# Contractions over 448 rows on TensorE: three full chunks and two half chunks that share one slot

## The chip, the cores and the metric

One core of a Trainium2 chip runs the whole program. The metric is device time in microseconds (us) of one execution. Runs of different kernels are compared on the same chip in the same rounds. Engines are written as in the profile: PE is the matmul engine (TensorE), PEld its weight loads, DVE, ACT and POOL are the vector, scalar and general engines, SP issues most DMAs. "L667" is a line of the kernel file; the line numbers of two versions differ.

## The reference, cut to what matters

```python
x: (1, 2048, 448)            # bf16 everywhere
h  = x + attn(layernorm(x))  # 16 heads of 28; query s sees keys s, s-2, ..., s-14
# attn: qkv = xn @ wqkv (448 x 1344);  o @ wo (448 x 448)
z  = gelu(layernorm(h) @ w_in)        # 448 -> 1792
z1, z2 = z[..., :896], layernorm(z[..., 896:])
g  = w_sp (2048 x 2048) @ z2 + b_sp   # the spatial matmul
h2 = h + (z1 * g) @ w_out             # 896 -> 448
```

Five of these matmuls contract over 448 rows: q and k, V, the output projection of attention ("y" below), z2 and z1. One matmul instruction of this program contracts over at most 128 rows.

## The kernel before

The program is a list of tasks. A list scheduler inside the kernel file gives each task an engine and a place in that engine's order, from priorities and from cost formulas written in the file. What it emits is a fixed order per engine, with semaphore waits; an engine never skips a task that has to wait. PSUM is a pool of eight banks.

448 rows are cut into four chunks of 112. One task makes one output in one bank:

```python
DC = 112; NCH = 4
def qk_tile(tc, g8, prio):               # q or k of 512 tokens, four heads
    b = Buf(P_bank)
    G.add([("pe", pe_us(4, 512))], [
        lambda e, c=c: e.matmul(bank(b, 512), wsrc[:, c, gg, :], xhT[0:DC, c, col0:col0 + 512],
                                start=(c == 0), stop=(c == NCH - 1)) for c in range(NCH)], ...)
    G.add([("act", ...), ("dve", ...)], [... copy the bank to qT or kT ...])
# V of one attention block, y_block, a half of z2 and z1_tile are made the same way:
#   four matmuls of 112 rows, 448 columns (V, y, z2) or 512 columns (q, k, z1)

def att_block(i):                        # 18 blocks of 114 queries
    # V; scores: 16 matmuls of 32 rows, four at a time in the array (tile_position=(hh * 32, 0));
    # exp on ACT; mask on DVE; attention times V on PE; divide on DVE; transpose on PE
def y_block(m):                          # 16 blocks; ... then residual, layernorm, transposes
    G.add([("pe", pe_us(4, D))], [
        lambda e, c=c: e.matmul(bank(b, D), qT[0:DC, c, PAD + lo:PAD + hi], wo_sb[:, c, :],
                                start=(c == 0), stop=(c == NCH - 1)) for c in range(NCH)], ...)
```

The z2 matmuls may start only after the last attention block's first exponential (`after=[exps[-4]]`), the z1 matmuls only after its last one (`after=[last_exp]`), because ACT changes its function table there once (in the trace one table load of 1.28 us, at 91.19 us).

The softmax here doesn't subtract the row's maximum and nothing guards it: scores larger than these inputs give would overflow.

## Time and profile before

| | us |
|---|---|
| median of 4 runs | 265.51 (265.35 to 266.02) |
| span of the profiled run | 263.0 |
| PE busy | 255.1, 97% of the span |
| share of PE in the chain of waits | 89% |

From the page of the kernel before: busy time by engine, then the busy share (in tenths) of 40 slices of 6.6 us for PE, DVE, ACT and the granted PE clock, then the chain that ended last.

```profile
PE 255.1 (97%) x1868; PEld 129.8 (49%) x1868; DVE 152.4 (58%) x342; ACT 106.3 (40%) x204; POOL 46.6 (18%) x123
...
PE   6899999999998999999999999999999999999995
...
DVE  4697999979979999999431333131513133222233
ACT  1468979779979976772011000111010100010100
...
PEclk9999999999999999999999999999999999999999
...
PE 89%; DMA 3%; DVE 3%; ACT 2%; SPq 1%; POOL 1%; issue 0%; DVEq 0%
```

PE is the bound: it is busy in nearly every slice, and the chain of waits runs along it. DVE and ACT are nearly as busy until slice 17 (about 115 us), where attention and the z2 normalisation are over.

The next view gives busy time and instruction counts by stretches of time. I cut at four events seen in the trace: first transpose, first z2 matmul, first z1 matmul, end. So the lines are start, attention, z2, and the rest (z1, spatial matmul, last projection).

```profile
core 0: us, PE busy (x) PEld busy (x) DVE busy (x) ACT busy (x) POOL busy (x), PEclk, DMA share, GB/s
0.00:9.51 9.51, 7.38 (x29) 3.13 (x29) 4.23 (x14) 3.09 (x5) 7.09 (x31) 1.00 0.82 204
9.51:87.61 78.10, 75.53 (x961) 44.64 (x960) 70.76 (x163) 63.94 (x131) 22.80 (x51) 1.00 0.43 89
87.61:117.51 29.90, 29.90 (x212) 16.53 (x210) 29.73 (x77) 22.01 (x41) 12.45 (x32) 1.00 0.25 49
117.51:263.00 145.49, 142.31 (x673) 65.47 (x671) 47.73 (x92) 17.26 (x29) 4.27 (x11) 1.00 0.20 45
```

The price of a change of array mode can be read off PE's order of time (start, length, engine, line, operation; the ends of matmuls are modelled, the starts are what to read). The first line is the last of four full q/k matmuls, the second a group of 32-row score matmuls:

```profile
26.30 0.38 PE L524 MATMUL psum<-xhT,early 112*128 112x512 bf16 x1
26.62 0.38 PE L547 MATMUL psum<-qT,kT 32*128 32x114 bf16 x16
26.93 1.04 PE L524 MATMUL psum<-xhT,early 112*128 112x512 bf16 x4
```

A 512-column matmul that is followed by another of its kind has the next start 216 ns later; here it is 0.31 us. The whole score group takes 0.31 us; sixteen matmuls of 114 columns, four side by side, would stream in about 0.2 (their starts come in fours, 39 to 51 ns apart).

The last reading is the end of the attention stage, again in PE's order of time; the bracket is idle time of PE and what ended it. L535 is V, L547 the scores, L632 the first z2 matmul.

```profile
81.03 0.92 PE L535 MATMUL psum<-early,xhT 112*124 112x448 bf16 x4
...
82.27 0.38 PE L547 MATMUL psum<-qT,kT 32*128 32x114 bf16 x16
83.64 0.38 PE L547 MATMUL psum<-qT,kT 32*128 32x114 bf16 x16 [0.98 <-ACT E L556]
...
86.89 0.44 PE L547 MATMUL psum<-qT,kT 32*124 32x110 bf16 x16 [0.20 <-ACT E L556]
...
87.61 0.92 PE L632 MATMUL psum<-w_in,xhT 112*128 112x448 bf16 x4
```

After the last V block (81.03) three score groups remain, and PE begins z2 6.6 us later.

### The profile page before, as it was taken

To read this page: it belongs to the slowest core of one execution; us is meant where nothing else is said; L and a number is where in the kernel's file an instruction comes from. 1 tells how busy PE (TensorE), PEld (TensorE's weight loads), DVE (VectorE), ACT (ScalarE), POOL (GpSimd) and SP (SyncE) were. 2 spreads that over 40 slices of the span, in tenths; PEclk is the share of its full clock that TensorE was granted. 3 is DMA by queue.
4 is the path that set the end of the run, shared out by engine and by line. 5 is a ranking of instruction groups with operands and counts; after the bars stand their busy time and mean duration, and the time that the engine had idled before them with its cause. 6 is when DMAs were issued, how large, how long until landed. Compare 5 with 4: busy or idle time off the path is not lost.

```text
span 263.0 us, 4647 instructions
## 1 busy us (share of the span) xinstructions
PE 255.1 (97%) x1868; PEld 129.8 (49%) x1868; DVE 152.4 (58%) x342; ACT 106.3 (40%) x204; POOL 46.6 (18%) x123
## 2 busy tenths in 40 slices
PE   6899999999998999999999999999999999999995
PEld 2445665556655555554444444444544444444442
DVE  4697999979979999999431333131513133222233
ACT  1468979779979976772011000111010100010100
POOL 8676013221211125555000000000000000000000
PEclk9999999999999999999999999999999999999999
DMA  6999945000001213213000344401445200200002
GB/s 172 325 261 241 137 99 66 2 0 2 2 0 24 62 43 44 54 42 49 12 0 0 70 98 98 125 4 38 101 100 84 70 0 0 72 0 0 0 2 70
DMA packets 42182, 16.91 MB, mean 64 GB/s; under 512 B 35248, under 2 KB 41584, under 8 KB 42160
## 3 DMA queue, kind: packets, MB, share of 16 engines
q1 hardware_dynamic: 42160, 16.61, 29.3%
q8 instruction: 15, 0.25, 0.4%
q14 instruction: 7, 0.06, 0.1%
HBM read 6.37 MB, written 1.84 MB: 31 GB/s over the span
## 4 chain that ended last, share of the span: by engine, by line
PE 89%; DMA 3%; DVE 3%; ACT 2%; SPq 1%; POOL 1%; issue 0%; DVEq 0%
PE psum L667 37%; PE psum L524 10%; PE psum L632 9%; PE psum L654 9%; PE psum L685 8%; PE psum L596 4%; PE psum L535 4%; DMA x_tm<-in_A_x_dram 3%; PE psum L496 2%; PE psum L569 2%; PE psum L547 2%; ACT E L556 2%; PE psum L582 1%; DVE st L486 1%; DVE tring L491 1%; SPq L440 0%
## 5 line engine op out<-in xcount | busy, mean ns | idle before, releaser
L672 DVE TENSOR_TENSOR ub<-psum,bb 128x512 bf16<-128x512 f32 x28 | 19.4, 691 | 82.7 <-PE psum L667 82.7
L659 ACT ACTIVATE z1p<-psum 128x512 bf16<-128x512 f32 x28 | 16.7, 597 | 114.1 <-PE psum L654 114.1
L667 PE MATMUL psum<-wsp,z2p 128*128 128x512 bf16 x224 | 51.0, 379 | 0.0
L667 PE MATMUL psum<-early,z2p 128*128 128x512 bf16 x224 | 50.8, 379 | 0.0
L556 ACT ACTIVATE E<-psum 128x456 bf16<-128x456 f32 (+1 forms) x72 | 35.0, 562 | 1.4 <-PE psum L547 1.2
L667 PEld LDWEIGHTS psum<-wsp,z2p 128*128 128x128 bf16 x224 | 21.8, 98 | 26.5
L667 PEld LDWEIGHTS psum<-early,z2p 128*128 128x128 bf16 x224 | 21.9, 98 | 26.4
L524 PE MATMUL psum<-xhT,early 112*128 112x512 bf16 x128 | 30.5, 379 | 0.1
L654 PE MATMUL psum<-xhT,w_in 112*128 112x512 bf16 x112 | 28.8, 378 | 0.0
L514 POOL TENSOR_TENSOR rstd<-va,mhalf 128x1 f32<-128x1 f32 x48 | 27.7, 580 | 3.2
L512 POOL TENSOR_SCALAR va<-mv 128x1 f32<-128x1 f32 x48 | 13.2, 283 | 72.8 <-DVE mv L488 62.0
L632 PE MATMUL psum<-w_in,xhT 112*128 112x448 bf16 x128 | 25.5, 352 | 0.0
L685 PE MATMUL psum<-w_out,z1p 128*128 128x448 bf16 x112 | 21.8, 352 | 0.0
L486 DVE BATCH_NORM_STATS2 st<-x_tm 128x6 f32<-128x448 bf16 x32 | 19.2, 610 | 2.6 <-DMA x_tm<-in_A_x_dram 2.5
L637 ACT ACTIVATE z2p<-psum 128x448 bf16<-128x448 f32 x32 | 17.1, 544 | 7.2 <-PE psum L632 7.2
L564 DVE TENSOR_TENSOR E<-E,maskb 128x1824 bf16<-128x1824 bf16 (+1 forms) x18 | 19.6, 1089 | 0.0
L640 DVE BATCH_NORM_STATS2 st<-z2p 128x6 f32<-128x448 bf16 x32 | 18.1, 596 | 0.0
L654 PEld LDWEIGHTS psum<-xhT,w_in 112*128 112x128 bf16 x112 | 10.9, 97 | 13.3
L524 PEld LDWEIGHTS psum<-xhT,early 112*128 112x128 bf16 x128 | 11.5, 97 | 12.0 <-ACT V L508 0.2
L632 PEld LDWEIGHTS psum<-w_in,xhT 112*128 112x128 bf16 x128 | 12.1, 98 | 10.3
L535 PE MATMUL psum<-early,xhT 112*128 112x448 bf16 (+1 forms) x72 | 16.1, 352 | 0.8 <-DVE xhT L509 0.8
L685 PEld LDWEIGHTS psum<-w_out,z1p 128*128 128x128 bf16 x112 | 11.0, 98 | 10.4
(59 smaller groups left out, 245.7 us busy)
## 6 DMA issues: line engine op xcount, KB each, us to landing
out_dram<-tring SPq DMA_DIRECT2D x16, 112.0 KB, 1.8
w_in<-in_B_w_in_dram SPq DMA_DIRECT2D x1, 1568.0 KB, 13.8
x_tm<-in_A_x_dram SPq DMA_DIRECT2D x1, 896.0 KB, 10.0
early<-in_A_wqkv_dram SPq DMA_DIRECT2D x1, 784.0 KB, 6.0
w_out<-in_B_w_out_dram SPq DMA_DIRECT2D x1, 784.0 KB, 15.5
bb<-in_B_b_sp_dram SPq DMA_DIRECT2D x1, 512.0 KB, 13.2
wsp<-in_B_w_sp_dram SPq DMA_TRANSPOSE x32, 2.8
early<-in_B_w_sp_dram SPq DMA_TRANSPOSE x32, 2.7
```

Of the source, the lines that this page charges most:

```text
L486: G.add([("dve", dve_us(D))], [lambda e: e.bn_stats(st[:, s.slot, 0:6], x_tm[:, m, :])], [r_x[m]], [s], [s], prio=prio)
L514: G.add([("pool", 0.61)], [lambda e: e.tensor_tensor(rstd[:, k:k + 1], va[:, k:k + 1], mhalf[:, 0:1], ALU.pow)], [r_va[k], r_half], [r_rs[ ...
L524: lambda e, c=c: e.matmul(bank(b, 512), wsrc[:, c, gg, :], xhT[0:DC, c, col0:col0 + 512], start=(c == 0), stop=(c == NCH - 1)) for c in ra ...
L535: lambda e, c=c: e.matmul(bank(b, D, 0, nk), xhT[0:DC, c, t0:t0 + nk], stg[:, c, 2 * D:3 * D], start=(c == 0), stop=(c == NCH - 1)) for c ...
L556: lambda e, hh=hh: e.activation(E[0:nk, ev.slot, hh * 4:(hh + 1) * 4, 0:nq], bank(lb[hh], 512, 0, nk).rearrange("p (g c) -> p g c", c=128) ...
L564: lambda e: e.tensor_tensor(E[0:nk, ev.slot, :, 0:nq], E[0:nk, ev.slot, :, 0:nq], maskb[0:nk, mi:mi + 1, 0:nq].to_broadcast([nk, NHEAD, nq ...
L632: lambda e, c=c, b=b, h=h, m=m: e.matmul(bank(b, D), xhT[0:DC, c, PAD + 128 * m: PAD + 128 * m + 128], w_in[:, c, FH + D * h: FH + D * (h ...
L640: lambda e, h=h, m=m, s=s: e.bn_stats(st[:, s.slot, 6 * h:6 * h + 6], z2p[:, m, D * h:D * (h + 1)])],
L654: lambda e, c=c: e.matmul(bank(b, 512), w_in[:, c, fc * 128:(fc + 1) * 128], xhT[0:DC, c, PAD + 512 * tc: PAD + 512 * (tc + 1)], start=(c ...
L667: lambda e, s=s: e.matmul(bank(b, 512), z2p[:, s, fc * 128:(fc + 1) * 128], w[:, s, :], start=(s == 0), stop=(s == NB - 1)) for s in range ...
L672: G.add([("dve", dve_us(512))], [lambda e: e.tensor_tensor(ub[:, u.slot, :], bank(b, 512), bb[:, 512 * tc:512 * (tc + 1)], ALU.add)], [b, ...
L685: lambda e, f=f: e.matmul(bank(b, D), z1p[:, f, 128 * m:128 * m + 128], w_out[:, f, :], start=(f == 0), stop=(f == FC7 - 1)) for f in rang ...
```

## The change

448 is 3 x 128 + 64. The intent: make six full 128-row matmuls for two outputs, and put their two 64-row remainders into the upper and lower half of the array, at the same time. Two outputs take seven slots (a slot is the time of one full matmul: 216 ns with 512 columns, 189 with 448) where they took eight. One switch into the half-array mode and back is called a trip below. For that, q and k of one tile, two V blocks, the two halves of a z2 block and two z1 tiles become one task with two banks. Chunk 3 starts at row 320, so it overlaps chunk 2; each half of the array finds its 64 rows in place.

```diff
-DC = 112
+CH0 = (0, 128, 256, 320)
+        def pair(b, ws, xs, n, m=128):
+            fns = []
+            for j in range(2):
+                for c in (0, 1, 2 + j):
+                    fns.append(lambda e, j=j, c=c: e.matmul(bank(b[j], n, 0, m[j]), ws(j, ALL, c), xs(j, ALL, c),
+                                                            start=(c == 0), stop=False))
+            for j, ps, c in ((1, LO, 2), (0, HI, 3)):
+                fns.append(lambda e, j=j, ps=ps, c=c: e.matmul(bank(b[j], n, 0, m[j]), ws(j, ps, c), xs(j, ps, c),
+                                                               start=False, stop=True, tile_position=(ps.start, 0)))
+            return fns
+        def pair_us(n):
+            return pe_us(7, n) + 0.15
-                for isk in (0, 4):
-                    qk_tile(tc, g + isk, pos(4 * tc) - 3.0 + 0.3 * g)
+                qk_pair(tc, g, pos(4 * tc) - 3.0 + 0.3 * g)
  ... V: v_pair(i, ...) for blocks i and i + 1; z2: both halves of block m; z1: z1_pair for tiles tc and tc + 1 ...
         def y_block(m):
             G.add([("pe", pe_us(4, D))], [
-                lambda e, c=c: e.matmul(bank(b, D), qT[0:DC, c, PAD + lo:PAD + hi], wo_sb[:, c, :],
+                lambda e, c=c: e.matmul(bank(b, D), qT[HI if c == 3 else ALL, c, PAD + lo:PAD + hi],
+                                         wo_sb[HI if c == 3 else ALL, c, :],
  ... weights are loaded by two DMAs each (rows 0 to 383, rows 320 to 447); transposes make 128-row chunks ...
```

y has no partner for its remainder: its fourth matmul has 64 rows and a slot to itself. The scheduler is told seven slots and 0.15 us for a pair, and for y nothing beyond its four slots.

## The prediction

> **What bounds the kernel now.** PE: busy 97% of the 263.0 us span on the page, 89% of the chain of waits. Its busy times are modelled, so I took start-to-start times of neighbouring matmuls from the trace: 216 ns for 512 columns, 189 for 448, 56 for a transpose, the same at 112 contraction rows as at 128. Summed over the program's order this is about 244 us. The rest is mostly the start (first transpose at 9.5 us) and about 4 us of real idle time: 1.8 us before 14.7 us (x loads and DVE), 2.2 us at 82 to 88 us (ACT). From there to the end PE has no gap. DVE and ACT are 80 to 100% busy until about 90 us (windows of 10 us), but PE seldom waits for them.
>
> **What the change saves.** A pair of outputs took eight full slots; now six, plus one in which two 64-row matmuls run side by side. There are 30 pairs of 512 columns (16 q/k, 14 z1) and 25 of 448 (9 V, 16 z2): at best 30 x 216 + 25 x 189 ns = 11.2 us. That the halves overlap I take from the 32-row score matmuls, where four start within 10 ns.
>
> **What it adds.** The Trainium skill (TensorEngine Tiling (Array Packing), Tiling Modes, Key Properties) says that changing the tiling mode drains TensorE. The trace agrees and gives the price at the score matmuls: the last full matmul before them takes 312 ns to the next start instead of 216 (284 instead of 189); on the way back 138 ns where streaming takes 48; then 10 ns more in the first full matmul. One trip costs about 95 + 90 + 10 = 195 ns. Each pair makes one: a 512-column pair gains 20 ns, a 448-column pair loses 6. The output projection (L596, 16 blocks) gets a 64-row fourth chunk without partner: a full slot as before, plus a trip, 16 x 0.19 = 3.1 us lost. Four pairs run straight into score matmuls and share a switch (-0.4 us). Walking the changed PE order with these durations gives 246.6 against 244.3 us: **+2.3 us**, nearly all in the attention stage.
>
> **Other effects.** Weights load with 14% more bytes and one more issue each (0.45 us on the SP queue), so first weights and x blocks 4 to 7 land 0.5 to 1 us later, but q/k pairs now run earlier and fill PE's first waits. Both outputs of a pair finish together: evictions come in bursts, which may add stalls before 90 us; or the new order removes the wait at 82 us. I allow +0.2 us, spread about 2 us. Transposes, evictions, spatial matmul and last projection stay.
>
> **Prediction.** 268 us, 8 in 10 between 264.5 and 272. Faster by over 2%: 0.05; within: 0.80; slower: 0.15.
>
> **What would show it.** Trace: about 310 ns from a 512-column pair's last full matmul to its halves, 4 ns between the halves, 305 ns to the next full matmul; a pair 1.71 us against 1.73. Output projection 0.95 us per block against 0.76. PE gapless after 90 us; z2, z1 and spatial stages as long as before within 1 us.
>
> **What would make it wrong.** Halves not side by side (+11 us); a 64-row switch cheaper than a 32-row one (50 ns per trip is 3.5 us over 71 trips); PE starved in the attention stage by the new order.

## More of the kernel before

An execution of this program can have its TensorE clock halved for a few microseconds in the middle. The records show it as a mean granted clock of 0.981 to 0.987 (0.994 where it lasts half as long) instead of 0.998 to 1.000.

## The result, and the profile after

The changed kernel takes 276.1 us (median of 4, 275.51 to 276.11) against 265.51 before: 1.039 times as long, interval 1.037 to 1.041. (Ratios are the mean time of one kernel's fast runs over that of the other's in the same rounds, so not quite the ratio of the medians.) The prediction of 268, range 264.5 to 272, was wrong. The output is correct.

The page of the changed kernel, the same lines:

```profile
PE 260.7 (95%) x1846; PEld 119.8 (44%) x1868; DVE 158.4 (58%) x354; ACT 96.0 (35%) x192; POOL 45.0 (16%) x123
...
PE   6789999999998799999999999999999999999995
...
PEclk9999999999999779999999999999999999999999
...
PE 89%; DVE 5%; ACT 2%; issue 1%; POOL 1%; DVEq 0%; POOLq 0%
```

New here: the clock row falls to 7 tenths in two slices (13 and 14, 89 to 103 us), and PE is under 90% in slices 12 and 13 (82 to 96 us), where before it was so in slice 12 alone.

By stretches, cut at the same four events:

```profile
0.00:11.01 11.01, 8.88 (x28) 3.47 (x29) 3.96 (x13) 3.26 (x5) 7.37 (x31) 1.00 0.84 272
11.01:96.33 85.32, 77.84 (x952) 39.60 (x960) 76.27 (x174) 57.24 (x119) 19.93 (x50) 0.98 0.36 79
96.33:129.26 32.93, 32.77 (x211) 13.79 (x210) 29.95 (x77) 19.47 (x40) 12.96 (x32) 0.94 0.23 44
129.26:274.40 145.14, 141.23 (x659) 62.97 (x670) 48.25 (x93) 16.06 (x30) 4.75 (x11) 1.00 0.18 42
```

| stage | before, us | after, us | difference |
|---|---|---|---|
| start | 9.51 | 11.01 | +1.5 |
| attention | 78.10 | 85.32 | +7.2 |
| z2 | 29.90 | 32.93 | +3.0 |
| z1, spatial, last projection | 145.49 | 145.14 | -0.35 |

The last row has the 14 z1 pairs, and it moved as predicted (14 x 20 ns = 0.28 us). A z1 pair in PE's order of time:

```profile
152.34 1.46 PE L532 MATMUL psum<-xhT,w_in 128*128 128x512 bf16 x6
153.73 0.39 PE L535 MATMUL psum<-xhT,w_in 64*128 64x512 bf16 x2
154.06 1.25 PE L699 MATMUL psum<-wsp,z2p 128*128 128x512 bf16 x5
```

From its start to the next task's start are 1.71 us (predicted 1.71; two outputs took 1.73 before). Single starts in the trace give the parts: 310 ns from the last full matmul to the first half, 4 ns between the halves, 319 ns from there to the next full matmul, whose own successor comes 10 ns late. A 448-column pair takes 1.54 us (predicted 1.52, before 1.51), a y block 0.97 us against 0.76 (predicted 0.95). So the halves do run side by side, and the two mode switches cost nearly what the score matmuls said (319 ns on the way back, where 305 was predicted). That half of the prediction holds.

The end of the attention stage, where the time went (L579 scores, L601 attention times V, L532 full matmuls of pairs: V's at 80.81, z2's at 96.33):

```profile
80.81 1.31 PE L532 MATMUL psum<-early,xhT 128*128 128x448 bf16 x6
...
84.13 0.38 PE L579 MATMUL psum<-qT,kT 32*128 32x114 bf16 x16
...
86.29 0.38 PE L579 MATMUL psum<-qT,kT 32*128 32x114 bf16 x16 [0.30 <-DVE x_tm L632]
...
88.35 0.56 PE L601 MATMUL psum<-V,E 128*128 128x29 bf16 x16 [0.38 <-DVE E L596]
89.10 0.38 PE L579 MATMUL psum<-qT,kT 32*128 32x114 bf16 x16 [0.19 <-ACT E L588]
...
90.88 0.38 PE L579 MATMUL psum<-qT,kT 32*128 32x114 bf16 x16
91.99 0.56 PE L601 MATMUL psum<-V,E 128*128 128x29 bf16 x16 [0.73 <-DVE E L596]
...
95.20 0.67 PE L579 MATMUL psum<-qT,kT 32*124 32x110 bf16 x16
...
96.33 0.95 PE L532 MATMUL psum<-w_in,xhT 128*128 128x448 bf16 x2
```

The last V pair starts at 80.81, as early as the last V block did before. But now five score groups remain after it, not three, and PE reaches z2 only 15.5 us later. In that stretch PE has nothing to do but the attention blocks' own short matmuls, and waits for the steps of each block on DVE and ACT.

In the same stretch the granted clock falls. Windows of 3.41 us, aligned to its change:

```profile
86.40:89.81 3.41, 2.51 (x56) 1.33 (x49) 3.35 (x9) 2.91 (x8) 0.79 (x2) 1.00 0.39 83
89.81:93.22 3.41, 2.03 (x45) 1.46 (x46) 2.95 (x7) 3.22 (x8) 1.57 (x2) 1.00 0.17 38
93.22:96.64 3.42, 3.31 (x42) 1.77 (x40) 2.62 (x8) 2.20 (x5) 0.00 (x0) 0.50 0.20 47
96.64:100.05 3.41, 3.41 (x11) 0.99 (x9) 2.19 (x5) 1.11 (x3) 0.79 (x2) 0.50 0.33 73
```

In the second line PE is busy for 2.03 us by modelled ends. I worked out from the start times how long it really streamed, counting each matmul's columns at 2.4 GHz (the clock that the Trainium skill gives in TensorE: Matmul & The Clock Gate, Part 1; 512 columns then take 213 of the 216 ns measured) and simultaneous ones once: 0.34 of the window. (22 of 1868 matmul records are missing from this trace; e14, the same kernel with a full record, shows that none of them belongs here.) Then follow 6.83 us, two such windows, at half clock; z2 begins near the middle of them. No two matmul starts in the thin window are more than 0.94 us apart.

### The profile page after: what moved, and what is told of

It is laid out like the page before. It is cut to its first block, busy times and chain, and to the rows that moved or that the text cites. A ratio compares the mean times of both kernels' runs of the same rounds, so it can differ in the third digit from the quotient of the medians.

```text
span 274.4 us, 4632 instructions
## 1 busy us (share of the span) xinstructions
PE 260.7 (95%) x1846; PEld 119.8 (44%) x1868; DVE 158.4 (58%) x354; ACT 96.0 (35%) x192; POOL 45.0 (16%) x123
## 3 DMA queue, kind: packets, MB, share of 16 engines
HBM read 6.83 MB, written 1.84 MB: 32 GB/s over the span
## 4 chain that ended last, share of the span: by engine, by line
PE 89%; DVE 5%; ACT 2%; issue 1%; POOL 1%; DVEq 0%; POOLq 0%
PE psum L699 36%; PE psum L532 25%; PE psum L717 8%; PE psum L535 6%; PE psum L628 5%; PE psum L489 3%; PE psum L506 2%; PE psum L601 2%; PE psum L614 1%; ACT E L588 1%; DVE st L496 1%; DVE tring L501 1%; DVE x_tm L632 1%; PE psum L579 1%; DVE xhT L519 1%
## 5 line engine op out<-in xcount | busy, mean ns | idle before, releaser
L699 PE MATMUL psum<-early,z2p 128*128 128x512 bf16 x219 | 48.6, 379 | 0.3
L691 ACT ACTIVATE z1p<-psum 128x512 bf16<-128x512 f32 x28 | 15.2, 594 | 86.1 <-PE psum L535 86.1
L522 POOL TENSOR_SCALAR va<-mv 128x1 f32<-128x1 f32 x48 | 11.7, 248 | 88.0 <-DVE mv L498 75.3
L532 PE MATMUL psum<-xhT,early 128*128 128x512 bf16 x87 | 21.6, 379 | 3.1 <-DVE tring L501 1.2
L532 PE MATMUL psum<-w_in,xhT 128*128 128x448 bf16 x96 | 22.0, 368 | 0.0
L532 PE MATMUL psum<-xhT,w_in 128*128 128x512 bf16 x81 | 20.1, 379 | 0.3 <-issue 0.2
L596 DVE TENSOR_TENSOR E<-E,maskb 128x1824 bf16<-128x1824 bf16 (+1 forms) x18 | 19.5, 1081 | 0.3 <-ACT E L588 0.3
L518 ACT ACTIVATE qT<-psum 128x512 bf16<-128x512 f32 (+1 forms) x20 | 11.7, 584 | 18.1 <-PE psum L535 11.0
L628 PE MATMUL psum<-wo,qT 128*128 128x448 bf16 x64 | 17.5, 374 | 0.0
L721 DVE TENSOR_TENSOR tring<-psum,x_tm 128x448 bf16<-128x448 f32 x16 | 9.3, 620 | 11.2 <-PE psum L717 11.2
L532 PEld LDWEIGHTS psum<-xhT,early 128*128 128x128 bf16 x96 | 8.2, 97 | 11.1 <-ACT V L518 1.0
```

What stands on the lines that cost most here:

```text
L532: fns.append(lambda e, j=j, c=c: e.matmul(bank(b[j], n, 0, m[j]), ws(j, ALL, c), xs(j, ALL, c), start=(c == 0), stop=False))
L596: lambda e: e.tensor_tensor(E[0:nk, ev.slot, :, 0:nq], E[0:nk, ev.slot, :, 0:nq], maskb[0:nk, mi:mi + 1, 0:nq].to_broadcast([nk, NHEAD, nq ...
L628: lambda e, c=c: e.matmul(bank(b, D), qT[HI if c == 3 else ALL, c, PAD + lo:PAD + hi], wo_sb[HI if c == 3 else ALL, c, :], start=(c == 0), ...
L699: lambda e, s=s: e.matmul(bank(b, 512), z2p[:, s, fc * 128:(fc + 1) * 128], w[:, s, :], start=(s == 0), stop=(s == NB - 1)) for s in range ...
```

## The experiments

My theory after reading the traces was ORDER: the tasks of twice the size lead to another fixed order, in which PE lacks work at the end of the attention stage. Its rivals: SWITCH or TRIPS (the half tiles and their mode switches cause the whole loss, through waits that they set off), and PLAN (the order was planned on wrong costs, nothing for a trip of y, so that PE falls behind the order that all engines follow, and waits follow from that). Apart from these stands the clock dip, as a consequence or by chance. Fifteen runs were made. e1 to e4, e5 to e8 and e9 to e15 each shared the runs of the kernel before (7, 7 and 12 runs; the three sets ran on three chips). The differences of 1 to 5 us below are read from means of runs that agree about the dip.

### e1: the pairing alone

```diff
 # kernel before, 112-row chunks; q+k, two V blocks, two z2 halves, two z1 tiles as one task each
+            for j in range(2):
+                for c in range(NCH):
+                    fns.append(lambda e, j=j, c=c: e.matmul(bank(b[j], n, 0, m[j]), ws(j, ALL, c), xs(j, ALL, c),
+                                                            start=(c == 0), stop=(c == NCH - 1)))
+            return pe_us(8, n)
```

> The kernel before (four chunks of 112 rows, no half tiles, no mode switches) with only the pairing of the change: q with k, two V blocks, two z2 halves, two z1 tiles are each one task that takes two PSUM banks at once. PE work is the same as before. Theory ORDER (what was lost beyond the switches comes from the paired tasks and the static order they lead to: PE waits in the attention stage): 268 to 272 us, PE waits before the z2 stage up by 2 us or more. Theory SWITCH (the half tiles and their mode switches cause all of the loss, and pairing by itself is free): 265.5 us within 1.

272.52 us (271.89 to 273.33), all four with the dip; the kernel before in the same rounds 268.7 with the dip and 265.3 to 266.1 without. So the pairing costs 3.9 us (dip against dip, means 272.57 and 268.71) with no half tile in the program. The weight loads are those of the kernel before, too. SWITCH falls: a large part of the loss has nothing to do with half tiles. The time lies just above the expected 268 to 272 us, which did not foresee the dip.

### e2: y's fourth chunk in full

```diff
-   qT[HI if c == 3 else ALL, c, PAD + lo:PAD + hi], wo_sb[HI if c == 3 else ALL, c, :]
+   qT[:, c, PAD + lo:PAD + hi], wo_sb[:, c, :]      # wo_sb[0:64, 3, :] set to zero, rows 384..447 in wo_sb[64:128, 3, :]
```

> The changed kernel with the fourth chunk of the output projection as a full 128-row matmul (64 rows of its weights are zero), so 16 of the 71 trips to the half-array mode are gone and nothing else. If a trip costs its 0.19 us on a chain that PE bounds: 276.1 - 3.1 = 273 us. Theory PLAN (the static order was planned with no trip in the output projection, PE falls behind that plan, and the waits follow from it): most of the loss goes, 267 to 269 us. Theory ORDER: 272 to 274 us, with the attention stage still some 4 us longer than before.

269.13 us (268.61 to 269.99); three of four without the dip. That looked like PLAN, at 7 us for 16 trips. But the added memset and another DMA changed the order too (four score groups after the last V pair instead of five), so it is not a clean test. e9 repeats it in an unchanged order.

### e3: true costs for the scheduler

```diff
-            return pe_us(7, n) + 0.15
+            return pe_us(7, n) + 0.195
-            G.add([("pe", pe_us(4, D))], [          # y_block
+            G.add([("pe", pe_us(4, D) + 0.195)], [
```

> The changed kernel with only the scheduler's PE costs corrected to what the trace showed: 0.195 us per trip instead of 0.15 in a pair and instead of nothing in the output projection. The instructions are the same, their order differs. Theory PLAN: the waits of PE in the attention stage go, and the switches alone stay: 268 to 269 us. Theory ORDER or SWITCH: 275 us or more.

270.05 us (269.35 to 270.78), all without the dip: between the two expectations. The same instructions in another order are 5 to 6 us faster than the changed kernel (274.96 us in e14, on another chip, and 276.1 in the first runs); about 2.5 us of that are the dip. Only three score groups remain after the last V pair, as in the kernel before. The order alone is thus worth several microseconds, and the cost that the scheduler was not told is a part of it. What is left, +4.4 us against the three dip-free runs of the kernel before in these rounds (265.7), is more than the 2.3 us of the trips.

### e4: pairs with half tiles in z2 and z1 only

```diff
 # attention as before; layernorm 2 transposes to 128-row chunks; z2 and z1 in pairs as in the change
+            n = 128 if i else DC
+            c0 = CH0 if i else [c * DC for c in range(NCH)]
```

> Attention stage of the kernel before (112-row chunks, unpaired, unchanged order), and the pairs with half tiles only in z2 and z1; the second layernorm's transposes make 128-row chunks. All theories: a trip of 195 ns against a saved slot of 189 or 216 ns gives 16 x 6 - 14 x 20 ns = -0.2 us, so 265.3 us within 0.7, and no drop of the granted clock. A result over 266.5 us would say that the half tiles cost more in the later stages than their start-to-start times show.

265.41 us (265.23 to 266.03; mean 265.52), no dip, against 265.68 (mean of three dip-free runs) before. As expected: outside the attention stage the change is worth nothing, and costs nothing.

### e5: four outputs per trip, in z2 and z1

```diff
+            for j in range(4):
+                for c in (0, 1, 2 + j % 2): ...            # twelve full matmuls
+            for k in range(0, 4, 2):
+                for j, ps, c in ((k + 1, LO, 2), (k, HI, 3)): ...   # two slots of halves, one trip
```

> Attention stage of the kernel before; in z2 and z1 four outputs share one trip: twelve full matmuls, then two slots of halves side by side, instead of sixteen slots. If a trip costs 195 ns and the halves of one pair follow the other's without a new drain: 7 x (2 x 216 - 195) + 8 x (2 x 189 - 195) = 3.1 us saved, less up to 1 us for the larger tasks where z2 starts: 262.5 to 263.5 us, faster than both kernels. If halves on the same rows of the array can't follow one another without a wait, 264.5 us or more.

Two runs without the dip: 263.93 and 264.31 us; two with a clock of 0.981 at 269.0 (left out). Against 264.95 before (three dip-free runs) it is 0.8 us faster, not 2 to 3: a miss. The grouped trip works as expected (see e12), but a z2 task of two blocks starts only when both blocks' transposes are done, and the trace shows z2 beginning 2.0 us later than before (89.64 against 87.61; 0.4 us of it was there from the start of the execution), with two PE waits of 0.5 and 0.6 us after that by the start times. Most of the saving was given back there; that the larger task is the reason is what the trace suggests, and no run tested it.

### e6: e2 and e3 together

> The changed kernel with both repairs: the output projection's fourth chunk in full (16 trips fewer) and the scheduler told 0.195 us per trip in a pair. If the loss is trips plus an order planned on wrong costs, 265.5 to 267.5 us: the pairs alone are worth nothing, and cost little. If pairing itself starves PE in the attention stage whatever the costs, as in e1, 269 us or more.

269.21 us (268.7 to 270.05), no dip. The trips of y are gone and the costs are right, and still it is 4.3 us slower than the dip-free kernel before (264.95). PLAN alone falls here: pairs cost something even in an order planned for them.

### e7: filler, to hold the clock

```diff
+        def fill(b, col0):        # two 256-column matmuls into a part of the bank that is overwritten or not read
+            return [lambda e, k=k: e.matmul(psum[:, b.slot * 512 + col0:b.slot * 512 + col0 + 256], ident[:, :],
+                                            w_in[:, k, 0:256]) for k in range(2)]
 # ahead of the transposes and attention-times-V matmuls of the last six blocks; order on all engines unchanged
```

> The changed kernel in its own order on every engine, with about 30 useless matmuls of 256 columns (0.11 us each) ahead of transposes and attention outputs in the last six blocks; their results are overwritten or not read. If the granted clock fell to half at 93 us because PE streamed for only 0.34 of the 3.4 us window before (0.43 was not enough to lower it), the drop goes, the z2 stage is some 2.5 us shorter (32.9 to about 30.4 us), and the attention stage gains less than the filler adds or loses up to 2 us: 272 to 276 us. If the drop has another cause, it stays, and the time is 276 to 279 us.

276.53 us with a dip of one window (clock 0.994; the window before it streamed for 0.34) and 275.31 us without any. The filler stands on the blocks' own path and costs about what the clock gives back, and one window stayed thin. It is consistent with the theory that a thin window brings the dip, and settles nothing; e14 does better.

### e8 and e13: V pairs alone, q/k pairs alone, without half tiles

```diff
 # e8:  e1 with q and k as in the kernel before
 # e13: e1 with V as in the kernel before
```

> The kernel before with only V blocks (and z2, z1, which cost nothing in e4) paired; q and k as before, no half tiles. If it is V's pairing that leaves PE without work at the end of the attention stage (in e1 four score groups were left after the last V block, before three), 269 to 272 us with the last V block early; if it is q/k pairing, 265.5 to 266.5 us.

> The kernel before with only q/k pairs (and z2, z1) and no half tiles; V blocks one by one as before. If both pairings starve PE, 267 to 268 us in executions without a clock drop (265.2 us before); if V's pairing is the cause alone, 265 to 266 us, and two to three score groups left after the last V block.

e8: 267.67 us (267.51 to 268.44), no dip; +2.9 on its dip-free runs before (mean 267.82 against 264.95). e13: 267.44 and 268.3 without the dip, +2.6 on 265.31 before, and 269.07 and 269.62 with it, only +0.8 on the two runs before that have it too (268.51). So the price of q/k pairs rests on two runs in each state, and the states disagree. Both pairings cost something, and neither expectation that named one culprit holds. In both three score groups remain after the last V block, so the count of groups is not the whole of ORDER. Where e8 loses its time is read from its trace further below; e13's profiled run has the dip in the stretch in question and can't be read so.

### e9 and e10: the changed kernel in exactly its own order, with trips taken out

```diff
 # e9: y's fourth chunk with all 128 rows (64 counted twice: wrong on purpose, relative error 0.31)
-   qT[HI if c == 3 else ALL, c, ...], wo_sb[HI if c == 3 else ALL, c, :]
+   qT[:, c, ...], wo_sb[:, c, :]
 # e10: as e9, and every half of a pair as a full matmul in a slot of its own (wrong on purpose, 0.78)
-            for j, ps, c in ((1, LO, 2), (0, HI, 3)): ... tile_position=(ps.start, 0)
+            for j, c in ((1, 2), (0, 3)): ... ws(j, ALL, c), xs(j, ALL, c)
```

> The changed kernel in exactly its own order on every engine, with the output projection's fourth chunk as a full 128-row matmul: 64 rows are counted twice, so the result is wrong on purpose; times are what a right one would take. 16 trips fewer. If trips only add their own length: 276.1 - 3.1 = 273 us. If PE's lag behind the planned order is what makes the waits, the attention stage shortens by more than 3.1 us, and the time is 269 to 272 us; the clock may or may not drop.

> The changed kernel in exactly its own order, with every half as a full 128-row matmul in its own slot (wrong on purpose, as in e9): no half tiles, no trips but those of the score matmuls, PE's work back at that of the kernel before (244.3 us by the trace's durations). What is still lost against the kernel before is due to the order and the paired tasks alone. Theory ORDER: 4 us or more still lost in the attention stage. Theory TRIPS: within 1.5 us of the kernel before, in executions with the same clock.

I compared the plans of these kernels: every engine has the same tasks in the same order as the changed kernel (their traces agree). e9: 271.48 to 272.7 with the dip, 269.57 without. e10: 272.14 to 272.89 with the dip, 270.03 without. These stretches are of e10, without the dip in the profiled run; the lines are attention and z2:

```profile
10.08:93.15 83.07, 75.99 (x961) 44.21 (x960) 75.84 (x174) 57.27 (x120) 19.89 (x50) 1.00 0.36 85
93.15:122.92 29.77, 29.77 (x213) 16.55 (x210) 29.17 (x76) 19.05 (x38) 12.72 (x30) 1.00 0.24 49
```

Attention takes 83.07 us (78.10 before) with no half tile anywhere and PE's work as before; z2 takes 29.77, as before. This is ORDER with the change's weight loads and 128-row chunks, and without half tiles; e1, which has the loads and chunks of before, loses as much (3.9 us against 4.0 here, both with the dip). Its waits at the end of the stage, same view as above:

```profile
87.73 0.40 PE L506 MATMUL psum<-ident,tring 128*128 128x128 bf16 x4 [0.80 <-DVE tring L501]
...
89.68 0.56 PE L601 MATMUL psum<-V,E 128*128 128x29 bf16 x16 [0.73 <-DVE E L596]
...
93.15 1.11 PE L532 MATMUL psum<-w_in,xhT 128*128 128x448 bf16 x5
```

The same five score groups, the same waits on the mask (L596) and on the normalisation (L501).

### e11: y's trips in the order of before

```diff
 # kernel before; the fourth chunk of y cut to 64 rows (wrong on purpose, relative error 0.34)
-   qT[0:DC, c, PAD + lo:PAD + hi], wo_sb[:, c, :]
+   qT[0:64 if c == 3 else DC, c, PAD + lo:PAD + hi], wo_sb[0:64 if c == 3 else DC, c, :]
```

> The kernel before in exactly its own order, with the fourth chunk of the output projection cut to 64 rows, so that each of the 16 blocks makes a trip to the half-array mode and back (wrong on purpose: 48 rows are left out). If a trip adds its length on a chain that PE bounds: +3.1 us. If PE's lag in a fixed order costs more than itself: +4 us or more, and the clock drops more often than in the kernel before. If the order leaves slack: under +2 us.

268.29 us (268.21 to 268.58), no dip, +3.0 on 265.31: sixteen trips cost sixteen trips. With e9 (2.7 us less than the changed kernel in the same set of runs, e14) this ends PLAN as first put: with the order held, PE's lag costs its own length and no more. What wrong costs did was to choose a worse order (e3).

### e12 and e15: a version that beats both

```diff
 # attention as before; z2 as before in full chunks (zero rows in the weights of the fourth); z1 four outputs per trip
 # e12 also lets the first z2 block in earlier:
-   after=[exps[-4]]
+   after=[exps[-8 if m < 1 else -4]]
```

> The kernel before with z1 in groups of four outputs per trip (7 x (2 x 216 - 195) ns = 1.7 us saved), z2 unpaired in full chunks (zero rows in the weights), and the first z2 block let in four score groups' exponentials earlier, to give PE work at the end of the attention stage. 262 to 263.5 us, and no drop of the clock, since PE streams more in the window that is thin in the kernel before (265.3 us without the drop, 268.7 with it).

> e12 without the early z2 block. If its gain is the shared trip of z1, 263.5 to 264.2 us in executions without a drop, with drops (267 us) in some as in the kernel before; if the early z2 block was most of it, 265 us.

e12: 263.76 us (263.25 to 263.88, six runs), 0.992 of the time before (0.988 to 0.996), just outside the expected 262 to 263.5. e15: 264.0 us (263.55 to 264.49, six runs), 0.993 (0.989 to 0.997). None of the twelve executions dips, though for e15 some dips were expected. Against dip-free runs before (265.31, nine runs) the means are 1.7 and 1.3 us lower: the shared trip gives most; the 0.4 us of the early block are hardly beyond the scatter of the runs. Both are correct. The z1 group in e12, four outputs:

```profile
144.98 2.75 PE L545 MATMUL psum<-xhT,w_in 128*128 128x512 bf16 x12
147.66 0.60 PE L549 MATMUL psum<-xhT,w_in 64*128 64x512 bf16 x4
148.20 2.12 PE L693 MATMUL psum<-wsp,z2p 128*128 128x512 bf16 x9
```

From 144.98 to 148.20 are 3.22 us where four outputs took 3.45: 14 slots and one trip. The two pairs of halves follow each other 0.22 us apart with no new drain.

### e14: the changed kernel again

> The changed kernel unchanged. In its trace every position of a 3.4 us window finds one in which PE streams for less than 0.40 of it, in the kernel before 22% of the positions: if the clock falls after such a window, all executions show the drop (mean clock about 0.987, 275.5 to 276.5 us), and the kernel before some. If the drop came by chance of that one chip, some executions run at 272.5 to 273.5 us.

274.96 us (274.15 to 275.91, six runs), 1.035 times before (1.031 to 1.039), and all six with the dip; with the first four that is ten of ten. The kernel before dips in 11 of its 30 executions, two of them by one window only (the first four have no clock on record and are counted as dip-free by their times). The window before the dip and the first one in it, in this run:

```profile
88.03:91.45 3.42, 1.81 (x55) 1.22 (x54) 2.98 (x7) 3.42 (x9) 1.99 (x3) 1.00 0.33 74
91.45:94.86 3.41, 3.14 (x41) 1.66 (x41) 2.23 (x5) 2.19 (x5) 0.03 (x1) 0.50 0.20 43
```

By streaming time, the windows just before a dip had 0.34 (changed kernel), 0.31 (e1), 0.34 (e7), 0.30 (e9), 0.36 (e13) and 0.29 (e14); no other window outside a dip was followed by one, in any of the 17 traces (the thinnest: 0.38 and 0.41 in e10, 0.43 in the changed kernel, e2 and e9). Wherever one lays a 3.41 us window in the changed kernel's trace, some window has under 0.40; in the kernel before that is so for 22% of the positions. So in every trace on hand the dip follows a thin window, and whether a short thin stretch triggers it may depend on where the window falls. But 0.40 is not itself the limit: every position in e10's trace also has a window under 0.40, and that execution has none under 0.38 and no dip. Nor do the 22% fit the kernel before well, which dips in 11 of 30 executions. No run changed the thinness alone (e7 tried), so it is a cause that all traces support and none proves.

## Why the prediction was wrong, point by point

The e9 to e15 rounds give a path in single steps on one set of rounds (means; the dip-free e10 is one run):

| step | us | change |
|---|---|---|
| kernel before, no dip (9 runs) | 265.31 | |
| paired tasks in their order, all matmuls full (e10, no dip) | 270.03 | +4.7 |
| the same with the dip (e10, 3 runs) | 272.48 | +2.5 |
| halves of the pairs side by side (e9, dip, 3 runs) | 272.23 | -0.25 |
| y's fourth chunk as a 64-row trip (e14, dip, 6 runs) | 274.96 | +2.7 |

- **Price of a trip, and what a pair gains:** right. 310, 4 and 319 ns (310, 4 and 305 foretold), 1.71 us a pair. The sum of the trips was predicted at +2.3 us and measured at +2.5 (2.7 - 0.25; the 0.25 is within the scatter of e9 and e10).
- **z1, spatial, last projection:** right (145.14 against 145.49 us). **z2 within 1 us:** wrong in the changed kernel (+3.0), because of the clock; without the dip it is 30.2 us in e3 and 30.3 in e6. **PE gapless after 90 us:** wrong too; PE still waits until z2 begins at 96.33 (up to 0.93 us from start to start, at 91.05).
- **"I allow +0.2 us, spread about 2 us" for the order and the evictions:** this is the step that failed. I named the possibility ("PE starved in the attention stage by the new order") and gave it almost no size. It measured +4.0 us (e10 against before, both with the dip) to +4.7 (both without), in place of 0.2.
- **The granted clock:** not in the prediction. The traces of before showed 1.0 throughout, and I took that as given. The stretch at 82 to 88 us that I saw as 2.2 us of PE waits was close to tripping it, and in 11 of 30 executions did. Made longer by the order, it trips every time, for 2.5 us here and 3.2 in the kernel before (268.51 against 265.31).
- **The start:** predicted nearly unchanged, and the profiled run starts 1.5 us later. PE runs its warm-up at half clock until 7.9 us in the changed kernel and 4.8 before; over all traces this moment lies between 4.8 and 7.9 us, and another profiled run of the changed kernel (e14) has 6.1. The traces settle it: in all 17, whatever the kernel, the first transpose follows this moment (9.49 us where the clock rises at 4.81, 10.08 at 6.00, 11.01 at 7.89). So these 1.5 us go with the execution and not with the change.

Why does a paired order starve PE? What is shown: V pairs cost 2.9 us and q/k pairs 2.6 (0.8 between runs with the dip) without any half tile (e8, e13), the loss comes back as waits in the attention stage, and a re-planned order (e3) wins back several microseconds with the same instructions, about half of them the dip. What the traces suggest: V and q/k matmuls are the work with which PE bridges the steps of an attention block on ACT and DVE, and a pair spends two portions of it at once, when one was needed. The last V task starts at 79 to 84 us in every version, but where the order of the changed kernel leaves five blocks for after it, PE has no bridge for them; z2, which could be one, has to wait for the last block's first exponential. In trace after trace that interval, from the last V matmul to the first z2 matmul, goes with the number of score groups left: three groups 6 to 9 us (before, e3, e8, e11, e13), four 9 to 10 (e1, e2, e6), five 13 to 15 (changed kernel, e9, e10, e14); in the changed kernel, e1, e9, e13 and e14 part of it is at half clock.

How much of ORDER is that end can be read from the two traces without a dip, e10 and the kernel before, one execution of each. By start times as above, no matmul streams for 17.8 us of the attention stage in e10 and for 12.8 before. Of these 5.0 us, 3.4 lie after the start of the last V matmul, 1.0 before 17 us, where the first tasks wait for normalised blocks from DVE (0.96, 0.52 and 0.88 us, against 0.30 and 0.52), and 0.6 in between. In e8, with V pairs alone, the last part is 0.8 us shorter than before and the first two are 1.7 longer, so its loss has another place. Whether the two banks that a pair holds at once add to this stays open; I made no run that separates them.

The Trainium skill helped twice. TensorEngine Tiling (Array Packing), Tiling Modes, says that changing the mode drains TensorE; the trace agrees and priced it. TensorE: Matmul & The Clock Gate, Part 1, says that the array's clock is halved or full by how busy PE was in a free-running window of about 3.4 us; the 3.41 us steps of the dips agree, and their coming and going between executions of the kernel before fits a window that does not start with the program. I had read it and did not apply it to a stretch without a long gap.

## What to carry to other kernels

A trip into a tiled array mode cost about 0.2 us here, as much as the slot that one pair of halves saves; gather several pairs' halves behind one trip, and give an odd remainder zero rows in a full chunk rather than a trip of its own. In a program with a fixed order per engine, making tasks twice as large is a change of schedule: test it alone, without the arithmetic that motivated it, as e1 did. And look for the thinnest few microseconds of PE before and after a change, since they may cost a halved clock (2.5 to 3.2 us here) that no sum of durations shows.

## What the Trainium skill lacked or had wrong

- TensorEngine Tiling (Array Packing), Tiling Modes: it gives no price for the drain. Measured: 93 to 96 ns on the way in, 90 to 103 ns on the way out, about 10 ns in the first full matmul after it; a second pair of halves in the same mode follows 0.22 us later with no drain. With 512 columns, one lone pair of 64-row remainders gains about 20 ns, not a slot.
- TensorE: Matmul & The Clock Gate, "Why this matters for your kernels": it asks for no PE-idle gap over about 3 us. (The page's section "A second HAM failure mode: psum-queue depth-cycling" does say that frequent short idle times can make the clock oscillate, but gives no share.) Here the clock halved for 6.8 us with no two matmul starts more than 1.01 us apart (changed kernel and e9); what mattered was the share of a 3.41 us window in which PE streamed (worked out from start times): in 17 traces, all six windows with 0.36 or less were followed by the halved clock, and none of the others (0.38 or more). The line between 0.36 and 0.38 rests on this one program.
- The same page, Terms, puts the penalty at the throttled time times (1 - K/N), which makes 3.4 us of 6.83 us at half clock. Measured: 3.0, 3.7 and 3.2 us in the three sets of runs of the kernel before, which agrees, and less in the paired orders: 2.5 us (e10), 2.7 (e9), 1.5 (e13), each from one or two dip-free runs.
- The same page, Back-to-back issue gap, gives about 131 ns per 512-column matmul in a stream of weight loads and matmuls, and says that its formula N / 2.4 + 2.5 (216 ns) counts too much there. The traces here show 216 ns start to start in such streams, as the formula has it.
